# A planned instruction order for a spectral, soft-mixture and gated network: the planner gets other costs and a lock, weight conversions become twice as wide, and expert weights are loaded by POOL's queue

## The chip, the cores and the metric

The kernel runs on one core of one Trainium2 chip. A core has five engines that the text names as the profile does: PE (matrix products; PEld is its weight load), DVE (vector), ACT (scalar, with activation functions), POOL (GpSimd, elementwise work and DMA issue) and SP (used here only to issue DMAs). Each engine runs its own instructions in the order in which they were written and waits at an instruction until what it needs is ready. The metric is the time of one execution of the whole program in microseconds (us), the median of several runs. Before the change it is 1789.39 us, the median of 3 runs from 1787.84 to 1794.08 us.

## The reference

The reference has three parts, and all of it runs in one launch. `x` is 8 batches of 3072 tokens with 256 channels.

```
X  = rfft(x, axis=1);  Xr, Xi = X.real, X.imag
Yr = Xr @ w_r - Xi @ w_i + b_r;  Yi = Xr @ w_i + Xi @ w_r + b_i
Yr, Yi = soft threshold of both at lam = 0.01
x  = irfft(Yr + 1j*Yi, n=3072, axis=1).reshape(8*3072, 256)

logits = x @ phi                                  # 32 slots, 4 for each of 8 experts
d = softmax of logits over all 24576 tokens;  c = softmax over the 32 slots
slot_input = d.T @ x;  slot_out[e] = relu(slot_input[e] @ w1[e]) @ w2[e]
x = c @ slot_out

out = (silu(x @ w_gate) * (x @ w_val)) @ w_out    # 256 -> 1536 -> 256
```

The three weights `w_gate`, `w_val` and `w_out` come as 64-bit floats. The kernel reads them as pairs of 32-bit words, builds 32-bit floats from the bits on DVE and stores them to a scratch in DRAM.

## The kernel before

The program has two halves. The **first half** (the function `phase1`) goes through the 8 batches. For each batch it loads `x` (`load_x`, tiles `xq`), transforms it in two stages of matrix products (`stage_a` into `chan`, lines 623 and 628; `stage_c` from `chan` into `xg` and `sf`/`sg`, lines 645 to 686), multiplies by the complex weights in three products (`stage_b`, line 740, into the PSUM tiles `pb`), adds bias, thresholds (`after_b`, lines 793 to 812, tiles `r` and `yt`), and turns and spreads the result (`stage_q`, lines 838 to 864, tiles `yt` and `yi`). `stage_c` to `stage_q` go in three groups for each batch, so there are 24 groups. Then come the logits, the running column maximum, the exponentials and the sums over tokens that become the slots' inputs (`logits`, `slots`, lines 898 to 1171), and the softmax over slots (`combine`, lines 1187 to 1221), whose result goes to the DRAM scratch `c_scr`. A float32 value that goes into a fast matrix product is split in a rounded part and the rest; the rest is what the functions `lo`, `sum_lo`, `join` and `rest_w` compute or what POOL does for them.

Between these steps the first half converts the 64-bit weights (`narrow`, lines 1242 to 1284): load a piece of 256 columns into `cvi` (SP), build bits in three DVE instructions (`bits`, lines 1250 to 1252), square the high word on ACT (`size`, 1256), select on DVE (`value`, 1269), for `w_out` split the value (ACT 1272, POOL or DVE 1279), and store it (SP, 1284). There are 36 pieces, and `cvi` and `cv` have one buffer each, so a piece can only begin when the store of the one before has been read out of `cv`.

The order of all this isn't written by hand. `Plan.add` takes a task with its engine (or a choice of POOL and DVE), an assumed duration, a rank, the tiles that it reads and writes, and buffers that it takes. `Plan.run` then picks, again and again, the ready task that can start first on its engine; among equals the one with the lower rank. It adds `LAG` where a task follows one of another engine, and models SP's issue and the transfers for tasks with `bus`. The picked order is the order of the instructions in the program. Ranks get an offset from the table `SHIFT`. Nothing of the plan's times is in the program: only the order, and for the tasks with a choice the engine.

At the **end of the first half** the last batch has nothing beside it: after its last `stage_b` PE fills its waits with products of the identity (`hold`, line 1454, 80 of them), while the chain `stage_q`, `logits`, `slots` of the last batch goes from engine to engine. The expert weights `w1` (8 transfers of 1 MB, line 467) and `w2` (8 of 1 MB, line 472) are issued by SP as soon as the regions of the tiles `x`, `chan` and of the weights' splits are free, and so are two of the three loads of the converted gate weights (`wg`, line 480). In the **passage** (`after_slots`, lines 1476 to 1573) the sums are folded (1487 to 1494), the experts computed (1502 to 1525), and gate and value weights multiplied with their output (1587). The **second half** is one steady loop from line 1600 on: 576 steps of a gate product, a value product, silu, multiply, split and six products into the output.

## Time and profile before

| | |
|---|---|
| time of the program, median of 3 runs | 1789.39 us (1787.84 to 1794.08) |
| time of the profiled execution | 1793.57 us |
| its span, first to last instruction | 1791.4 us |
| PE busy over the span | 1710.6 us (95%) |
| DVE busy | 1329.6 us (74%) |
| ACT busy | 981.4 us (55%) |
| POOL busy | 275.0 us (15%), nearly all in the first half |
| mean granted TensorE clock | 0.983 |

A row of the view by stretches gives the stretch, then the busy time of each engine with its number of instructions, the granted clock, the mean share of the DMA engines and the GB/s. A row of the timeline gives start, duration, engine, line, operation, the tile written and the tiles read, how many were merged, and in brackets how long the engine had been idle before and what ended it. Idle time counts only on the engine whose work ends last in that stretch.

### The profile page before, as it was taken

What the parts mean: (1) busy time and instruction counts of PE and PEld (TensorE: products, weight loads), DVE (VectorE), ACT (ScalarE), POOL (GpSimd) and SP (SyncE); (2) the same over time, 40 slices, a digit from 0 to 9 for tenths busy, and PEclk for the clock granted to TensorE, in tenths of its full rate; (3) what the DMA queues carried; (4) which work ended last, traced back from release to release, by engine and by line L of the source; (5) the groups of instructions that cost most, each with busy time, mean ns of one, the idle gap of its engine ahead of it and who ended that gap; (6) DMA issues with size and microseconds to landing.
All of it is one profiled execution on the core that took longest, in us unless ns stands there. A gap on an engine that the chain in (4) does not pass through costs nothing.

```text
span 1791.4 us, 23405 instructions
## 1 busy us (share of the span) xinstructions
PE 1710.6 (95%) x8266; PEld 1300.9 (73%) x8266; DVE 1329.6 (74%) x2222; ACT 981.4 (55%) x1833; POOL 275.0 (15%) x254
## 2 busy tenths in 40 slices
PE   6999999899989777999999999999999999999998
PEld 3665676566757563788888888888888888888886
DVE  4688979888887652677777777777777777777776
ACT  1654556445556412566666555566666655566664
POOL 1334344334443432000000000000000000000000
PEclk9999999999999888999999999999999999999999
DMA  9357464573736479012112112113112113111111
GB/s 178 72 110 143 89 142 104 110 150 84 152 88 171 148 237 286 13 24 51 24 24 50 25 24 51 24 24 51 25 25 51 25 25 51 24 25 25 25 25 27
DMA packets 258915, 134.43 MB, mean 75 GB/s; under 512 B 197392, under 2 KB 246256, under 8 KB 258800
## 3 DMA queue, kind: packets, MB, share of 16 engines
q1 hardware_dynamic: 252944, 120.37, 31.6%
q0 software_dynamic: 5856, 12.58, 4.0%
q8 instruction: 65, 1.06, 0.3%
q14 instruction: 50, 0.41, 0.1%
HBM read 69.99 MB, written 37.75 MB: 60 GB/s over the span
## 4 chain that ended last, share of the span: by engine, by line
PE 81%; DVE 12%; DMA 1%; issue 1%; SPq 1%; ACT 1%; POOL 0%; DVEq 0%; ACTq 0%
PE o L1628 45%; PE pg L1603 7%; PE pv L1604 7%; PE pb L740 7%; PE ac L623 4%; PE ac L645 3%; PE ch L1100 1%; DVE yt L854 1%; PE ch L1152 1%; PE ch L838 1%; DVE xg L667 1%; DVE cv L1251 1%; DVE chan L628 1%; DVE vpad L884 1%; PE pb L1454 1%
## 5 line engine op out<-in xcount | busy, mean ns | idle before, releaser
L1628 PE MATMUL o<-hh,wo 128*128 128x512 f32 x2304 | 723.4, 395 | 0.0
L1608 DVE TENSOR_TENSOR h<-sg,pv 128x512 f32<-128x512 f32 x576 | 394.0, 684 | 273.5 <-ACT sg L1606 271.7
L1606 ACT ACTIVATE sg<-pg 128x512 f32<-128x512 f32 x576 | 344.8, 599 | 423.4 <-PE pg L1603 423.4
L1628 PEld LDWEIGHTS o<-hh,wo 128*128 128x128 f32 x2304 | 434.9, 189 | 100.9
L1628 PE MATMUL o<-hl,wo 128*128 128x512 f32 x1152 | 454.2, 394 | 0.0
L1616 DVE TENSOR_TENSOR hl<-h,hh 128x512 fp32r<-128x512 f32 x576 | 393.6, 683 | 0.1
L1615 ACT ACTIVATE hh<-h 128x512 fp32r<-128x512 f32 x576 | 359.3, 624 | 0.8 <-DVE h L1608 0.7
L1628 PEld LDWEIGHTS o<-hl,wo 128*128 128x128 f32 x1152 | 216.4, 188 | 51.9
L1603 PE MATMUL pg<-cst,gstk 96*128 96x512 f32 x576 | 228.6, 397 | 0.0
L1604 PE MATMUL pv<-cst,gstk 96*128 96x512 f32 x576 | 226.6, 393 | 0.9 <-DVE gstk L1590 0.7
L812 POOL TENSOR_TENSOR yt<-r,yt 128x512 f32<-128x512 f32 x92 | 119.3, 1297 | 249.0 <-ACT yt L803 194.3
L740 PE MATMUL pb<-xg,wh 128*128 128x512 f32 x384 | 148.2, 465 | 9.4 <-DVE xg L667 4.1
L1555 POOL DMA_DIRECT2D cst<-c_scr x24 | 13.6, 570 | 810.8 <-PE pv L1604 799.6
L1604 PEld LDWEIGHTS pv<-cst,gstk 96*128 96x128 f32 x576 | 109.9, 191 | 27.7 <-DVE gstk L1590 1.6
L1603 PEld LDWEIGHTS pg<-cst,gstk 96*128 96x128 f32 x576 | 108.2, 188 | 24.5 <-issue 0.5
L623 PE MATMUL ac<-xq,fwd 96*128 96x512 f32 x224 | 111.4, 606 | 4.6 <-DVE chan L628 2.4
L628 DVE STREAM_TRANSPOSE chan<-ac 128x512 f32<-128x512 f32 x128 | 88.7, 703 | 35.7 <-PE ac L623 32.7
L645 PEld LDWEIGHTS ac<-cm,chan 128*128 128x128 f32 x768 | 100.6, 200 | 17.7 <-issue 6.4
L645 PE MATMUL ac<-cm,chan 128*128 128x128 f32 x768 | 105.6, 288 | 3.2 <-DVE xg L667 1.7
L740 PEld LDWEIGHTS pb<-xg,wh 128*128 128x128 f32 x384 | 68.0, 193 | 48.6 <-issue 19.6
L667 DVE TENSOR_TENSOR xg<-ac,xg 128x512 fp32r<-128x512 f32 x96 | 64.9, 680 | 23.7 <-ACT sf L670 14.8
L740 PE MATMUL pb<-xg,wl 128*128 128x512 f32 x192 | 77.1, 401 | 0.0
(146 smaller groups left out, 1633.1 us busy)
## 6 DMA issues: line engine op xcount, KB each, us to landing
yi<-yt SPq DMA_DIRECT2D x384, 64.0 KB, 2.1
out_dram<-ob SPq DMA_DIRECT2D x192, 128.0 KB, 2.8
xq<-in_x_dram SPq DMA_DIRECT2D x28, 768.0 KB, 7.2
cst<-c_scr POOLq DMA_DIRECT2D x24, 384.0 KB, 5.8
w1s<-in_moe_w_dram SPq DMA_DIRECT2D x8, 1024.0 KB, 7.5
w2s<-in_moe_w_dram SPq DMA_DIRECT2D x8, 1024.0 KB, 8.7
w_scr<-cv SPq DMA_DIRECT2D x48, 128.0 KB, 3.2
x<-in_x_dram SPq DMA_DIRECT2D x2, 1536.0 KB, 15.5
```

The lines of the kernel that those rows point to most:

```text
L623: nc.tensor.matmul(out=pt, lhsT=fwd[:, 8 - 8 * dh:136 - 8 * dh], rhs=T[kq][:, :, d1:d1 + 16], start=True, stop=True)
L628: nc.vector.transpose(out=chan[:, 12 * dh:12 * dh + 16, d0:d0 + 16, :].rearrange("p j d i -> p d j i"), in_=T[ka].rearrange("p n d -> p d n"),
L645: nc.tensor.matmul(out=pt[:, :, q:q + 2, i // 2, :], lhsT=chan[:, 16 * dh + j // 2, :, j % 2], rhs=cm[:, j, :].rearrange("p (c h k) -> p c ...
L740: nc.tensor.matmul(out=pt, lhsT=w[:, dh, m, es], rhs=xx, start=m != 1 and dh == 0 and n == 0, stop=dh == 1 and n == 2, skip_group_check=True,)
L812: e.tensor_sub(out=part(), in0=quarters(T[kr]), in1=part())
L1603: nc.tensor.matmul(out=pg, lhsT=gstk[:, 0, f * 128:(f + 1) * 128], rhs=rhs, start=True, stop=True)
L1604: nc.tensor.matmul(out=pv, lhsT=gstk[:, 1, f * 128:(f + 1) * 128], rhs=rhs, start=True, stop=True)
L1606: nc.scalar.activation(out=sg, in_=pg, func=AF.Silu)
L1608: nc.vector.tensor_mul(out=h, in0=sg, in1=pv)
L1615: nc.scalar.activation(out=hh, in_=h, func=AF.Copy)
L1616: nc.vector.tensor_sub(out=hl, in0=h, in1=hh.bitcast(F32))
L1628: nc.tensor.matmul(out=po_t[0][k], lhsT=w[:, f % 4, k * 128:(k + 1) * 128], rhs=a, start=(f == 0 and m == 0), stop=(f == NF - 1 and m == 2 ...
```

## The change

- **Costs.** A table `COST` replaces the durations that `add` is called with, by the name of the function, for nearly every task of the first half. Most DVE and ACT durations rise (0.6 to 0.68 for `stage_c.lo`, 0.6 to 0.71 for `stage_a.turn`). `LAG` falls from 0.25 to 0.07. `SHIFT` stays as it was.
- **Lock.** The names in `PAIR` are DVE tasks that the planner lets run only when no POOL task runs, and the reverse. This is a rule for the planned order; no wait is added to the program.
- **Wider conversions.** A piece has 512 columns: 18 pieces instead of 36. A piece of `w_out` takes 256 rows of 256 columns, two rows to a partition, and is stored with four DMAs.
- **Weights by POOL.** `w1` and `w2` are issued from POOL, and their tasks no longer wait for one another. The last `w2` is placed behind the last batch's first group; the loads `wg` wait for it in the plan.

```
+COST = {
+    "stage_c.lo": {"DVE": 0.681},
...
+    "narrow.rest": {"POOL": 1.28, "DVE": 0.68},
+}
+PAIR = {
+    "mix_w", "rest_w", "stage_c.sum_lo", "after_b.join", "logits.join", "logits.spread", "logits.newmax",
+    "slots.cross", "slots.rot", "slots.join", "narrow.bits", "narrow.value", "narrow.rest",
+}
...
-    LAG = 0.25
+    LAG = 0.07
...
-            "eng": eng if isinstance(eng, dict) else {eng: dur}, "rank": rank, "fn": fn, "bus": bus,
+            "eng": COST.get(name, eng if isinstance(eng, dict) else {eng: dur}),
+            "rank": rank, "fn": fn, "bus": bus, "pair": name in PAIR,
...
+        def pair(t, eng):
+            return not t["bus"] and (eng == "POOL" or eng == "DVE" and t["pair"])
...
-                    start = max(free.get(eng, 0.0), can)
+                    start = max(free.get(eng, 0.0), can, lock if pair(t, eng) else 0.0)
...
+            if pair(t, eng):
+                lock = stop
...
-        nc.sync.dma_start(out=w1_t[e], in_=w1[e].rearrange("(k p) f -> p k f", p=128))
+        nc.gpsimd.dma_start(out=w1_t[e], in_=w1[e].rearrange("(k p) f -> p k f", p=128))
...
-        nc.sync.dma_start(out=w2_t[e], in_=w2[e].rearrange("(k p) f -> p k f", p=128))
+        nc.gpsimd.dma_start(out=w2_t[e], in_=w2[e].rearrange("(k p) f -> p k f", p=128))
...
-                t = sb(chp, ki, [128, 256, 2], "cvi", dt=I32)
-                nc.sync.dma_start(out=t.rearrange("p c t -> p (c t)"), in_=src)
+                t = sb(chp, ki, [128, 512, 2], "cvi", dt=I32)
+                nc.sync.dma_start(out=t.rearrange("p (u c) t -> p u (c t)", u=src.shape[1]), in_=src)
...
-            add("SP", 0.06, rank, load, w=[ki], new=("cvi", ki), bus=0.73, after=[("ac", "a", b, 15)])
-            add("DVE", 1.1, rank + 0.3, bits, w=[ki, ka], new=("cv", ka))
+            add("SP", 0.06, rank, load, w=[ki], new=("cvi", ki), bus=1.46, after=[("ac", "a", b, 15)])
+            add("DVE", 2.0, rank + 0.3, bits, w=[ki, ka], new=("cv", ka))
...
-            for k in range(0, rows, 128):
-                for c in range(0, cols, 256):
+            for k in range(0, 256, 128):
+                for c in range(0, FD, 512):
...
+        for k in range(0, FD, 256):
+            two = [w[k:k + 256].rearrange("(u p) f -> p u f", u=2) for w in (w32, *w_scr[2:4])]
...
-                "SP", 0.06, TT - 2.5 + 0.1 * e, fetch_w1(e), r=["w1a" if e < 3 else "w1b"], w=[("w1", e)], bus=2.91,
-                after=[("w1", e - 2)] if e > 1 else [],
+            add("POOL", 0.6, TT - 2.5 + 0.1 * e, fetch_w1(e), r=["w1a" if e < 3 else "w1b"], w=[("w1", e)], bus=2.91)
+        add(
+            "POOL", 0.6, TT - 1.5, fetch_w2(E - 1), w=["w2x"], new=("yi", "w2x"), bus=2.91, after=[("yi", last, 0, 0)],
+        )
...
-                "SP", 0.06, TT + 0.1 * e, fetch_w2(e), r=["w2p"], w=[("w2", e)], bus=2.91,
-                after=[("w2", e - 2) if e > 1 else ("w1", e + 6)],
+            add("POOL", 0.6, TT + 0.1 * e, fetch_w2(e), r=["w2p"], w=[("w2", e)], bus=2.91)
```

Line numbers of the first half are higher by 89 to 91 after the change (DVE's line 1250 becomes 1340, PE's 1502 becomes 1593).

**DVE in the last batch's slots.** This is the stretch from the row maximum `rm` to the sums `rs`: `vt` is the turned product, `vpad` its rotation, `cv` a conversion. Before:

```order
L1187 TENSOR_REDUCE rm<-ls 96x32
L1250 TENSOR_SCALAR cv<-cvi 128x256
L1251 SCALAR_TENSOR_TENSOR cv<-cvi,cv 128x256
L1252 SCALAR_TENSOR_TENSOR cv<-cvi,cv 128x256
L1064 STREAM_TRANSPOSE vt<-ch 128x512
L884 TENSOR_TENSOR vpad<-vt,csm 128x16x24
L1269 SCALAR_TENSOR_TENSOR cv<-cvi,cv 128x128 x2
L1064 STREAM_TRANSPOSE vt<-ch 128x512
L884 TENSOR_TENSOR vpad<-vt,csm 128x16x24
L1199 TENSOR_REDUCE rs<-ls 96x32
```

After:

```order
L1277 TENSOR_REDUCE rm<-ls 96x32
L1154 STREAM_TRANSPOSE vt<-ch 128x512 x2
L974 TENSOR_TENSOR vpad<-vt,csm 128x16x24 x2
L1289 TENSOR_REDUCE rs<-ls 96x32
L1290 TENSOR_SCALAR rs<-rs 96x32
```

The conversion's four rows are gone from between `rm` and the second `vt`.

**DVE at the passage.** From the last batch's sum `acc` to the folded sums `tail`. Before:

```order
L1208 STREAM_TRANSPOSE vt<-ls 96x1024
L1171 SCALAR_TENSOR_TENSOR acc<-acc,fac,ch 128x258
L1250 TENSOR_SCALAR cv<-cvi 128x256
L1251 SCALAR_TENSOR_TENSOR cv<-cvi,cv 128x256
L1252 SCALAR_TENSOR_TENSOR cv<-cvi,cv 128x256
L1269 SCALAR_TENSOR_TENSOR cv<-cvi,cv 128x128 x2
L1250 TENSOR_SCALAR cv<-cvi 128x256
L1251 SCALAR_TENSOR_TENSOR cv<-cvi,cv 128x256
L1252 SCALAR_TENSOR_TENSOR cv<-cvi,cv 128x256
L1269 SCALAR_TENSOR_TENSOR cv<-cvi,cv 128x128 x2
L1490 COPY tail<-pst 128x64
L1493 TENSOR_SCALAR tail<-pr 128x1
```

After:

```order
L1179 TENSOR_TENSOR vpad<-vpad,p_5478 128x16x12 x4
L1298 STREAM_TRANSPOSE vt<-ls 96x1024
L1261 SCALAR_TENSOR_TENSOR acc<-acc,fac,ch 128x258
L1581 COPY tail<-pst 128x64
L1584 TENSOR_SCALAR tail<-pr 128x1
```

Two conversions stood between `acc` and `tail`; now none does, and in the whole program no conversion stands behind the last batch's `stage_c`.

**POOL at the end of the first half.** `p` is a product for the rotation, `ls` the logits' softmax, `yt<-r,yt` the threshold's join, `sg` the rest of a sum. Before (no loads of `w1` and `w2` are on POOL):

```order
L812 TENSOR_TENSOR yt<-r,yt 128x4x128 x4
L1279 TENSOR_TENSOR cv<-cv 128x256
L812 TENSOR_TENSOR yt<-r,yt 128x4x128
L1190 TENSOR_TENSOR ls<-ls,rm 96x1024
L884 TENSOR_TENSOR p_5620<-vt,csm 128x384 x2
L1279 TENSOR_TENSOR cv<-cv 128x256
L1204 TENSOR_TENSOR ls<-ls,rs 96x1024
```

After:

```order
L776 TENSOR_TENSOR sg<-sf,sg 128x4x64
L557 DMA w1s<-in_moe_w_dram 128x2x1024 x5
L902 TENSOR_TENSOR yt<-r,yt 128x4x128
L562 DMA w2s<-in_moe_w_dram 128x8x256
L902 TENSOR_TENSOR yt<-r,yt 128x4x128 x4
L562 DMA w2s<-in_moe_w_dram 128x8x256 x7
L1280 TENSOR_TENSOR ls<-ls,rm 96x1024
L974 TENSOR_TENSOR p_5478<-vt,csm 128x384 x2
L1294 TENSOR_TENSOR ls<-ls,rs 96x1024
```

Fourteen of the 16 loads now stand here, seven of them ahead of the last batch's `ls` and `p`. Over the whole program POOL has 95 rows of `sg` and 95 of `yt<-r,yt` (72 and 92 before) and DVE one of each (24 and 4 before).

## Rows read from the trace of the kernel before

**Rows 1.** Busy time by stretch: columns as told above, PE first.
```profile
38.00:624.00 586.00, 549.79 (x3070) 378.36 (x3070) 480.65 (x848) 312.80 (x637) 234.91 (x203) 0.97 0.55 119
624.00:666.00 42.00, 37.07 (x296) 31.16 (x294) 26.23 (x46) 10.13 (x18) 14.45 (x10) 0.92 0.71 215
666.00:681.00 15.00, 0.45 (x4) 0.20 (x8) 3.28 (x12) 1.71 (x4) 0.79 (x2) 0.54 1.05 349
...
711.00:1791.00 1080.00, 1073.80 (x4610) 869.44 (x4609) 796.08 (x1249) 643.33 (x1152) 10.01 (x18) 1.00 0.19 31
```

**Rows 2.** Timeline of PE, 645 to 689 us.
```profile
645.36 1.88 PE L1056 MATMUL ch<-td,csm 96*128 96x512 f32 x4
647.08 3.96 PE L1454 MATMUL pb<-ident 128*128 128x128 f32 x34
654.50 2.90 PE L1100 MATMUL ch<-vpad,csm 128*128 128x192 f32 x8 [3.46 <-DVE vpad L1089]
...
680.55 5.53 PE L1502 MATMUL ph<-w1s,tail 128*32 128x512 f32 x32 [14.86 <-DVE tail L1493]
...
686.59 1.92 PE L1502 MATMUL ph<-w1s,tail 128*32 128x512 f32 x16
```

**Rows 3.** Timeline of DVE, 664 to 681 us.
```profile
664.32 0.48 DVE L1171 SCALAR_TENSOR_TENSOR acc<-acc,fac,ch 128x258 f32<-128x258 f32 x1 [2.16 <-PE ch L1152]
...
678.56 0.29 DVE L1250 TENSOR_SCALAR cv<-cvi 128x256 int32<-128x256 int32 x1 [11.15 <-DMA w_scr<-cv]
...
680.27 0.22 DVE L1490 COPY tail<-pst 128x64 f32<-128x64 f32 x1
```

**Rows 4.** Timeline of SP's queue at 668 us (DMA issues).
```profile
668.40 4.20 SPq L1284 DMA_DIRECT2D w_scr<-cv  x2
```

**Rows 5.** Timeline of DVE in the last batch's slots.
```profile
648.47 0.71 DVE L1064 STREAM_TRANSPOSE vt<-ch 128x512 f32<-128x512 f32 x1
...
649.69 1.29 DVE L1269 SCALAR_TENSOR_TENSOR cv<-cvi,cv 128x128 f32<-128x128 f32 x2
```

**Rows 6.** Timeline of PE at 137 us: the product of 654.50 in an earlier batch.
```profile
137.86 1.57 PE L1100 MATMUL ch<-vpad,csm 128*128 128x192 f32 x8 [0.39 <-DVE vpad L1089]
```

**Rows 7.** Timeline of POOL, 628 to 646 us.
```profile
628.87 0.73 POOL L1279 TENSOR_TENSOR cv<-cv 128x256 f32<-128x256 f32 x1 [0.93 <-POOL yt L812]
...
645.90 1.91 POOL L1190 TENSOR_TENSOR ls<-ls,rm 96x1024 f32<-96x1024 f32 x1 [15.08 <-ACT td L1038]
```

**Rows 8.** One line at a time: count, duration ns min/median/max, first and last start.
```profile
L1251 DVE SCALAR_TENSOR_TENSOR cv<-cvi,cv x36: 424/426/2087, 39.4 to 678.9; 128x256 int32<-128x256 int32 x36
L1555 POOL DMA_DIRECT2D cst<-c_scr x24: 562/562/730, 693.0 to 1513.4; - x24
L1546 POOL DMA_DIRECT2D wo<-w_scr x6: 745/760/787, 694.9 to 700.4; - x6
```

**Rows 9.** Groups by line: busy us, mean ns of one, then idle before.
```profile
L1251 DVE SCALAR_TENSOR_TENSOR cv<-cvi,cv 128x256 int32<-128x256 int32 x36 | 24.5, 682 | 1.2
L1269 DVE SCALAR_TENSOR_TENSOR cv<-cvi,cv 128x256 f32<-128x256 f32 (+1 forms) x48 | 23.0, 499 | 0.3
L686 DVE TENSOR_TENSOR sg<-sf,sg 128x256 fp32r<-128x256 f32 x24 | 18.0, 758 | 7.6 <-ACT sg L682 7.5
L1252 DVE SCALAR_TENSOR_TENSOR cv<-cvi,cv 128x256 int32<-128x256 int32 x36 | 17.5, 486 | 1.2
L1250 DVE TENSOR_SCALAR cv<-cvi 128x256 int32<-128x256 int32 x36 | 15.8, 439 | 12.1 <-DMA w_scr<-cv 11.2 <-DMA cvi<-in_moe_w_gate_dram 0.9
L555 DVE SCALAR_TENSOR_TENSOR wmix<-wst 128x512 f32<-128x512 f32 x1 | 0.7, 685 | 0.0
```

**Rows 10.** What PE waited for, 38 to 624 us: total us, times, longest.
```profile
PE ch L1100 <- DVE vpad L1089: 8.5, 6, 5.0
PE pb L740 <- DVE xg L667: 4.1, 6, 1.0
```

**Rows 11.** Timeline of PE at the start.
```profile
26.51 1.98 PE L623 MATMUL ac<-x,fwd 96*128 96x512 f32 x4 [2.22 <-DVE chan L628]
```

More of the change, by code (lines that the diff above doesn't have):

```diff
@@ L286 @@
+PAIR = {
+    "mix_w",
+    "rest_w",
+    "stage_c.sum_lo",
+    "after_b.join",
+    "logits.join",
+    "logits.spread",
+    "logits.newmax",
+    "slots.cross",
+    "slots.rot",
+    "slots.join",
+    "narrow.bits",
+    "narrow.value",
+    "narrow.rest",
+}
 class Plan:
-    LAG = 0.25
+    LAG = 0.07
     HAND, SET, SEEN = 0.65, 0.9, 0.65
@@ L310, in add @@
     def add(self, eng, dur, rank, fn, r=(), w=(), new=None, bus=0.0, dmas=1, after=()):
-        name = [n for n in fn.__qualname__.replace("<locals>.", "").split(".")[-3:] if n not in ("go", "phase1")]
+        name = [n for n in fn.__qualname__.replace("<locals>.", "").split(".")[-3:] if n not in ("go", "phase1", "kernel")]
         name = ".".join(name[-2:])
@@ L1282, in store @@
                 af, pf = (T[(*ka, n)].bitcast(F32) for n in "ap")
-                for o, t in zip(dst, (pf,) if len(dst) == 1 else (af, pf)):
-                    nc.sync.dma_start(out=o, in_=t)
-            add("SP", 0.06, rank, load, w=[ki], new=("cvi", ki), bus=0.73, after=[("ac", "a", b, 15)])
-            add("DVE", 1.1, rank + 0.3, bits, w=[ki, ka], new=("cv", ka))
-            add("ACT", 0.3, rank + 0.3, size, w=[ki])
-            add("DVE", 0.36, rank + 0.3, value, w=[ki, ka])
+                if len(dst) == 1:
+                    nc.sync.dma_start(out=dst[0], in_=pf)
+                    return
@@ new lines, in store @@
+                for o, t in zip(dst, (af, pf)):
+                    t = t.rearrange("p (h u x) -> p u h x", h=2, u=2)
+                    for u in range(2):
+                        nc.sync.dma_start(out=o[:, u].rearrange("p (h x) -> p h x", h=2), in_=t[:, u])
+            add("SP", 0.06, rank, load, w=[ki], new=("cvi", ki), bus=1.46, after=[("ac", "a", b, 15)])
+            add("DVE", 2.0, rank + 0.3, bits, w=[ki, ka], new=("cv", ka))
+            add("ACT", 0.5, rank + 0.3, size, w=[ki])
+            add("DVE", 0.65, rank + 0.3, value, w=[ki, ka])
@@ L1290, in narrow @@
             if len(dst) == 2:
-                add("ACT", 0.3, rank + 0.3, part, w=[ka])
-                add({"POOL": 0.69, "DVE": 0.34}, 0, rank + 0.3, rest, w=[ka])
-            add("SP", 0.12, rank + 0.4, store, r=[ka], w=[("ws", i)], bus=0.37 * len(dst), dmas=len(dst))
+                add("ACT", 0.5, rank + 0.3, part, w=[ka])
+                add({"POOL": 1.23, "DVE": 0.6}, 0, rank + 0.3, rest, w=[ka])
+            add("SP", 0.12, rank + 0.4, store, r=[ka], w=[("ws", i)], bus=0.74 * len(dst), dmas=len(dst) ** 2)
@@ L1446, in phase1 @@
                 "SP", 0.12, TT + 0.9, fetch_wg(t), w=[("wg", t)], bus=2.91, dmas=2, new=("yt", ("wg", t)),
-                after=[("ws", i) for i, (_, d) in enumerate(jobs) if len(d) == 1] + [("yi", last, 2, 0), ("w2", E - 2)],
+                after=[("ws", i) for i, (_, d) in enumerate(jobs) if len(d) == 1] + [("yi", last, 2, 0), ("w2", E - 2), "w2x"],
             )
@@ L1460, in phase1 @@
             add(
-                "PE", 0.22, TT + 50, hold(i), w=[kh], new=("pb", kh) if i == 0 else None,
+                "PE", 0.224, TT + 50, hold(i), w=[kh], new=("pb", kh) if i == 0 else None,
                 after=[("pb", last, 2, eh, d, 0) for eh in range(2) for d in range(2)],
```

84 lines of the change are left out of this document (68 added, 16 removed).

## The prediction

> **What bounds the kernel now.** I read the busy time by stretches first. From 711 us on PE is busy 1073.8 of 1080 us at a granted clock of 1.00 [rows 1]; the change issues nothing there, so only the first 711 us can move. In 38 to 624 us, the body, PE is busy 549.8 of 586 us and DVE 480.7 (82%) [rows 1]: PE bounds, with 36.2 us in which it waits. From 624 to 666 us the last batch's chain runs alone, with identity products in PE's waits; from 666 to 681 us PE does 0.45 us of work [rows 1].
>
> The timeline of PE, read next, shows that hole as one wait of 14.86 us, put down to DVE's `tail` [rows 2]. The timeline of DVE says why: `acc` is done at 664.80, but `tail` begins at 680.27, because two pieces of the conversion stand between them in DVE's order, and the second waits 11.15 us for a store out of `cv` [rows 3]. SP issued those stores at 668.40 and took 4.20 us for two [rows 4], with the loads of `w2` ahead of them in its queue. Nothing in the passage needs that piece so early. So 14.86 us are a place in DVE's order, not a dependency.
>
> **The change part by part.** The profiled execution took 1793.57 us (span 1791.4 and 2.2 around it); the median shown is 1789.39, so 4.2 lower. The sum is made against the former and taken off the latter.
>
> *The hole.* No conversion stands between `acc` and `tail` any more. PE ended its own part 14.86 us before 680.55, at 665.69; after it come only `tail` and its two followers, 0.28 us by the same rows (680.27 to 680.55) [rows 2, 3]. So the experts' product starts at about 666.0: **-14.5 us**. What is late next is `wg`, needed only behind all of the experts' products. It is now issued right behind the softmax's stores, no longer behind `w2`; I cost it at nothing, and it would cost what it lands late.
>
> *The clock behind the hole.* The stretch 666 to 681 us shows a granted clock of 0.54, thus mostly the level of 1.2 GHz, and the first 32 of the experts' products take 5.53 us, while 16 later ones take 1.92 [rows 1, 2]. At the later pace 32 take 3.84, so up to 1.7 is won; without the wait I take **-1.5**.
>
> *The last batch's slots.* The first half of PE's product at 645.36 is done by about 646.3, but the first `vt` begins at 648.47, behind a conversion; a second conversion step holds DVE from 649.69 for 1.29 us [rows 2, 5]. Both are gone, up to 2.2 + 1.3 = 3.5 us. PE waits 3.46 us there [rows 2], but the order now puts 24 identity products after that product, where there were 17 (34 instructions, 3.96 us [rows 2]): 7 more are 1.6 us, and only **-1.8** is left. With that wait short, the 8 products that took 2.90 us at 654.50 can run as at 137.86, where they took 1.57 [rows 2, 6]; there are two such sets, so up to 2.6 is won, bounded below by nothing: **-2**.
>
> *The last join.* A conversion of 0.73 us on POOL stands ahead of the last join [rows 7]: **-0.7**.
>
> *The weights on POOL.* Sixteen issues come into POOL's order. The trace shows issues of 384 and 512 KB there, at 562 and 760 ns median [rows 8]; for 1 MB I estimate by that slope about 1 us, and at most twice 760 ns. Seven stand ahead of the last batch's `ls`: 7 to 10.6 us from about 631 (the last join, begun behind the conversion at 628.87, is over by then) to 642 at the latest. POOL sat idle for 15.08 us before 645.90 [rows 7], and that `ls` can come some 3 us earlier now: covered, **0**. If the cover went, `ls` and `p` would come late by up to 6. The five `w1` issues ahead of a join are some 3 to 5 us, with the same chance of being waited for; I leave them in the body's range. SP loses 16 issues and 18 of its piece loads, and keeps 36 piece stores of 48.
>
> The Trainium skill (SBUF — State Buffer, section "SBUF: two separate sides") warns that while DVE holds the port that it shares with GpSimd, POOL cannot write the descriptors of its DMAs. The rows speak against it here: the 24 issues of `cst`, nearly all in a stretch in which DVE is 74% busy, take 562 ns at the median and 730 at most [rows 1, 8]. By the rule each of the seven would wait for one DVE instruction; what that gives is a rival below.
>
> *The conversions.* Before, the four DVE lines cost 15.8 + 24.5 + 17.5 + 23.0 = 80.8 us [rows 9]. `L1251` shows what is in that: 424 ns at least, 2087 at most [rows 8]; the long ones overlap POOL's work. Undisturbed, a piece of 256 costs about 0.28 + 0.42 + 0.42 + 0.41 = 1.5 us, 55 for 36. A 512-wide step costs at most the 685 ns of `L555` [rows 9]; a piece then is about 0.5 + 3 x 0.685 = 2.5 us, 46 for 18. So DVE loses between 9 (only starts) and 35 us (waits too). POOL takes 23 more rests of sums; at 758 ns each [rows 9] DVE loses another 17. Together 26 to 52 of 481 us. None of it lies on PE's path by itself.
>
> *The order in the body.* This can't be summed from rows. What can be won is bounded by PE's 36.2 us of waits; 10 of the 15 listed pairs wait for DVE, together 26.5 us, the largest 8.5 and 4.1 [rows 10]. If DVE has up to a tenth less to do and the planned order keeps its pairs off POOL's work, I take some 30% of those 26.5: **-8**. The other end: ranks fitted to other costs now break other ties, and the new DVE costs are the profile's durations, in which neighbours overlap a little, so the planner thinks DVE slower than it is. I take +36 (PE's waits double) as that end, and -36 as the other; -8 is nearer to nothing than to either, since PE's own work there, 549.8 us, doesn't change.
>
> *The start.* DVE stops for the weights' sums after 8 transposes, not 7, and the rest of one split (`wl`) goes to POOL. PE waits 2.22 us there [rows 11]; one product is worth about 1 there (1.98 us for two, of two instructions each), the split's rest some more, and I take **-1.5** between 0 and -2.2.
>
> Sum: -14.5 - 1.5 - 1.8 - 2 - 0.7 - 8 - 1.5 = -30.0. On the profiled execution 1763.6, on the median 1759.4. The runs shown spread 6 us, and I set **1761 us**.
>
> **The rivals.**
>
> *Only the passage moves.* The body's waits stay at 36: the planner's better numbers are evened out by ranks that were not refitted, and the pairs still collide, since the lock is no wait in the program. Then DVE's short conversions lie beside a PE that was bound elsewhere. For it: DVE is not the bound; against: most of PE's waits name it. -30 + 8 = -22, about 1767; with a body worse by up to 14 it reaches 1781.
>
> *POOL becomes the gate (the slower side).* `r` has one buffer: ACT's next threshold waits until POOL's join has read it, and PE's next `stage_b` waits until ACT has emptied `pb`. POOL now has nearly every rest and join, each longer than DVE's, and loads in its queue that wait for a freed region with a join behind them. If in each of the 24 groups a POOL result comes later than PE needs it by x, the body grows by 24x. It outweighs -22 of the other terms and the 5.4 of the bound for "slower" from x = 1.14 us on; at x = 1.5 the time is 1789 - 22 + 36 = 1803. For it: POOL's join is in the chain of every group. Against: POOL is busy 234.9 of 586 us [rows 1], and a quarter more leaves it half idle.
>
> *The shared port holds the issues.* By the skill's rule above, each of the seven `w2` issues would wait for one DVE instruction, up to 1.2 us for the longest in that chain (two steps at 649.69 took 1.29 together [rows 5]): 8.4 us more on POOL, `ls` at about 650 and some 7 us later than needed; the hole's gain stays. -30 + 7 gives 1766. If instead POOL's queue cannot take 7 MB at once, POOL stands until part has been moved, at 349 GB/s [rows 1] 3 us per MB; three MB gives about the same.
>
> **How the numbers follow.** Forecast 0.60 (its own range 1747 to 1770), only the passage 0.22, the held issues 0.06, POOL as gate 0.10, a body better by over 20 us 0.02. The range 1743 to 1782 takes in the forecast, the held issues and nearly all of the passage alone; outside are the gate and the far ends, some 0.17. A run of this kernel can tell 0.3% (5.4 us) from no change: faster is below 1784. That holds for all but the gate and a small end of the passage case: faster 0.83; the gate splits into slower 0.10, and same has 0.07.
>
> **What would show it.** Right: in the new trace the experts' first product follows the folded sums within about 1 us, with no conversion behind the last `acc`; the 32 first products take under 4.5 us; PE's idle time in the body is below 36 us, and the body is some 8 us shorter; the `L1341` durations have a smaller spread over their least value. Wrong: a wait of PE above 2 us between 624 and 711 us that ends with a POOL instruction or with a landing of `w2` or `wg`; POOL's `ls` of the last batch late behind its DMA issues; or a body longer than 586 us, with ACT's waits for `r` or PE's for `pb` grown, in which case the gate's delay for each group decides how much of the passage's gain is left.

## The result and the profile after

The changed kernel takes 1768.97 us (median of 4 runs, 1767.65 to 1769.84), the kernel before 1788.62 us (4 runs beside it, 1787.76 to 1794.08): a ratio of 0.988, with a 95% interval from 0.9858 to 0.9902. That is 19.7 us faster, where 28 were forecast. One execution among all those below (of the kernel "last two pieces late, first try") took 2818.9 us at a granted clock of 0.557 and is left out of its median.

| | before | after |
|---|---|---|
| span of the profiled execution | 1791.4 us | 1768.0 us |
| PE busy over the span | 1710.6 us (95%) | 1704.9 us (96%) |
| DVE busy | 1329.6 us | 1276.0 us |
| POOL busy | 275.0 us | 307.8 us |
| first product of the first `stage_c` | 33.95 us | 34.81 us |
| end of the last `stage_b` product | 624.50 us | 615.27 us |
| first product of the experts | 680.55 us | 659.24 us |
| from there to the span's end | 1110.9 us | 1108.8 us |

The lines of the table split the difference of the spans, -23.4 us: the start +0.9, the body (590.5 to 580.5) -10.1, the passage from the last `stage_b` to the experts (56.1 to 44.0) -12.1, and everything behind that -2.1. Lines of the changed kernel are 89 to 91 higher than those of before.

The view by stretches of the changed kernel, to be read beside [rows 1]:

```profile
36.00:615.00 579.00, 546.80 (x3089) 373.46 (x3089) 438.80 (x765) 318.38 (x626) 264.61 (x238) 0.99 0.56 124
615.00:647.00 32.00, 31.41 (x261) 26.88 (x263) 19.20 (x34) 8.03 (x14) 16.70 (x14) 1.00 1.04 323
647.00:659.00 12.00, 3.99 (x42) 2.13 (x30) 0.53 (x2) 0.81 (x1) 4.08 (x2) 0.73 1.04 356
690.00:1768.00 1078.00, 1071.71 (x4609) 868.74 (x4607) 795.44 (x1248) 642.78 (x1150) 10.02 (x18) 1.00 0.19 31
```

In the body DVE is busy 42 us less and PE waits 32.2 us instead of 36.2. Over the exact bodies, first the kernel before and then the changed one, the same view gives:

```profile
33.95:624.50 590.55, 553.46 (x3098) 381.79 (x3098) 483.29 (x853) 314.98 (x642) 236.13 (x204) 0.97 0.55 119
34.81:615.27 580.46, 548.26 (x3100) 374.81 (x3099) 439.51 (x766) 318.44 (x626) 264.88 (x238) 0.99 0.56 124
```

So the 10.1 us are two halves: PE waits 32.2 us instead of 37.1, and its products take 548.3 us instead of 553.5, at a mean granted clock of 0.99 instead of 0.97. The steady half is as it was. But there is a hole again, from 647 to 659 us, and from 615 on the DMA engines are full (1.04). The timeline of PE shows which product waits (compare [rows 2]):

```profile
641.88 1.47 PE L1190 MATMUL ch<-vpad,csm 128*128 128x192 f32 x8
643.51 1.57 PE L1190 MATMUL ch<-vpad,csm 128*128 128x192 f32 x8
...
646.42 1.49 PE L1242 MATMUL ch<-yi,p 128*32 128x256 f32 x23
655.33 1.93 PE L1242 MATMUL ch<-yi,p 128*32 128x256 f32 x16 [7.42 <-DMA c_scr<-td]
...
659.24 5.32 PE L1593 MATMUL ph<-w1s,tail 128*32 128x512 f32 x32
...
665.08 1.92 PE L1593 MATMUL ph<-w1s,tail 128*32 128x512 f32 x16
```

The timeline of DVE shows what has become of the old hole [rows 3]:

```profile
657.32 0.48 DVE L1261 SCALAR_TENSOR_TENSOR acc<-acc,fac,ch 128x258 f32<-128x258 f32 x1 [10.66 <-PE ch L1242]
658.96 0.22 DVE L1581 COPY tail<-pst 128x64 f32<-128x64 f32 x1 [1.16 <-PE pst L1578]
```

Between `acc` and `tail` there are 1.16 us where there were 15; the old hole is gone. In its place the last 16 slot products wait 7.42 us. The releaser that stands there, `c_scr`, is a store that these products don't read. They read `yi`, and the line that issues `yi` (SP, 21 issues from 620 us on) has this:

```profile
L954 SPq DMA_DIRECT2D yi<-yt x21: 585/585/1077, 620.0 to 645.7; - x21
...
who waited for it (us, times):
  PEld ch L1242: 7.9, 1
...
DMA to landing us min/median/max: 9.2/9.8/10.6
```

Over the whole program before, `yi` landed in 2.1 us at the median; in the same stretch of that kernel (629 to 656 us, 18 issues, with `w2` in the same queue) it was 6.5, and nobody waited. Here seven `w2` of 1 MB run beside it, which POOL has handed over all at once, as its timeline shows:

```profile
620.85 6.14 POOL L562 DMA_DIRECT2D w2s<-in_moe_w_dram  x7
635.80 1.90 POOL L1280 TENSOR_TENSOR ls<-ls,rm 96x1024 f32<-96x1024 f32 x1 [8.80 <-ACT td L1128]
```

And the line of these issues, with its durations in ns:

```profile
L562 POOL DMA_DIRECT2D w2s<-in_moe_w_dram x8: 882/883/927, 607.5 to 626.1; - x8
```

POOL itself is not late: an issue costs 0.88 us, and `ls` still waited for ACT. What is left is the data; a run below tests that. The seven `w2` are not alone: the ten `yi` issued from 611.4 to 620.0 us, ahead of them, already took 9.0 us at the median, beside the five `w1` and one `w2` that POOL had issued from 602.65 us on.

### The profile page after: what moved, and what is told of

Its sections match the earlier page's. It is cut to its first block, busy times and chain, and to the rows that moved or that the text cites. A ratio compares the mean times of both kernels' runs of the same rounds, so it can differ in the third digit from the quotient of the medians.

```text
span 1768.0 us, 23212 instructions
## 1 busy us (share of the span) xinstructions
PE 1704.9 (96%) x8266; PEld 1292.7 (73%) x8266; DVE 1276.0 (72%) x2116; ACT 981.8 (56%) x1809; POOL 307.8 (17%) x292
## 4 chain that ended last, share of the span: by engine, by line
PE 89%; DVE 5%; ACT 2%; DMA 1%; issue 1%; SPq 1%; POOL 0%; DVEq 0%; ACTq 0%; POOLq 0%
PE o L1719 45%; PE pb L830 9%; PE pg L1694 8%; PE pv L1695 8%; PE ac L713 6%; PE ac L735 4%; PE ch L928 1%; PE pb L1545 1%; PE ch L1242 1%; PE ch L1054 1%; PE ch L1190 1%; PE ch L988 1%; PE ch L1146 1%; PE pg L1678 1%; SPq L673 0%
## 5 line engine op out<-in xcount | busy, mean ns | idle before, releaser
L902 POOL TENSOR_TENSOR yt<-r,yt 128x512 f32<-128x512 f32 x95 | 124.9, 1315 | 223.8 <-ACT yt L893 124.5
L1646 POOL DMA_DIRECT2D cst<-c_scr x24 | 13.5, 566 | 818.9 <-PE pv L1695 797.9
L718 DVE STREAM_TRANSPOSE chan<-ac 128x512 f32<-128x512 f32 x128 | 88.1, 702 | 38.1 <-PE ac L713 35.3
L757 DVE TENSOR_TENSOR xg<-ac,xg 128x512 fp32r<-128x512 f32 x96 | 65.4, 683 | 27.4 <-ACT sf L760 15.2
L776 POOL TENSOR_TENSOR sg<-sf,sg 128x256 fp32r<-128x256 f32 x95 | 71.0, 757 | 64.3 <-ACT sg L772 54.4
```

Source lines behind the costliest of these rows:

```text
L718: nc.vector.transpose(out=chan[:, 12 * dh:12 * dh + 16, d0:d0 + 16, :].rearrange("p j d i -> p d j i"), in_=T[ka].rearrange("p n d -> p d n"),
L902: e.tensor_sub(out=part(), in0=quarters(T[kr]), in1=part())
```

## The experiments

Three theories were open. *The lock*: the body gains because the planner keeps DVE's paired operations off POOL's. *The durations*: it gains because the planner knows better how long things take. *The widening*: it gains because DVE has less to do. And for the passage: the new wait is w2's data on POOL's queue, or it is something else.

All runs in one table, in the order of the text. "Body" is the time from the first `stage_c` product to the end of the last `stage_b` product, "passage" from there to the experts' first product, both from the profiled execution. Each ratio is to runs of the kernel before that were made beside that kernel; the medians of these lie between 1788.62 and 1790.75 us.

| kernel | median us | ratio to before (95%) | body | passage |
|---|---|---|---|---|
| before | 1788.62 | | 590.5 | 56.1 |
| changed | 1768.97 | 0.988 (0.9858 to 0.9902) | 580.5 | 44.0 |
| changed, no lock, old durations | 1794.98 | 1.0025 (1.0013 to 1.0038) | 604.5 | 44.1 |
| changed, no lock | 1807.60 | 1.0093 (1.0076 to 1.011) | 618.0 | 43.2 |
| changed, old durations | 1763.14 | 0.9849 (0.9829 to 0.9869) | 575.6 | 42.6 |
| before, wide conversions only | 1797.59 | 1.0038 (1.0023 to 1.0052) | 604.8 | 35.3 |
| before, lock only | 1778.09 | 0.9927 (0.9911 to 0.9942) | 587.1 | 39.2 |
| before, lock and wide | 1760.41 | 0.9841 (0.9816 to 0.9867) | 580.9 | 34.5 |
| changed, narrow conversions | 1775.20 | 0.9914 (0.9893 to 0.9935) | 588.3 | 43.6 |
| before, last two pieces late, first try | 1794.84 | 1.0029 (1.0015 to 1.0043) | 586.6 | 38.5 |
| before, last two pieces late, second try | 1793.85 | 1.0024 (1.001 to 1.0039) | 589.2 | 40.1 |
| changed, w2 late | 1775.28 | 0.9909 (0.9893 to 0.9926) | 581.0 | 35.8 |
| changed, three w2 late | 1766.76 | 0.987 (0.9846 to 0.9894) | 581.1 | 42.9 |
| changed, old durations, three w2 late | **1757.86** | 0.9809 (0.9788 to 0.983) | 576.2 | 38.0 |

The body's time has a spread of its own: the two kernels with the last pieces late have the same order of instructions as the kernel before up to 620 us, and the three bodies lie between 586.6 and 590.5 us.

### The lock and the durations

Three kernels fill the square of "lock or not" and "old or measured durations", all with wide conversions and POOL's queue. Without both (cuts are marked with `...`; durations that the change had altered in three other lines go back too):

```diff
-PAIR = {
-    "mix_w",
-    "rest_w",
...
-}
+PAIR = set()
...
-    LAG = 0.07
+    LAG = 0.25
...
-            "eng": COST.get(name, eng if isinstance(eng, dict) else {eng: dur}),
+            "eng": eng if isinstance(eng, dict) else {eng: dur},
```

> The changed kernel with the old durations of the planner, the old lag and no lock: wide conversions and weights by POOL's queue alone. Theory (of the body's 10.1 us most comes from DVE's conversions, 80.8 to 54.4 us of busy time, and little from the planner's better numbers; the hole goes by the widening too, since no piece is left over at the end): 1768 to 1774 us, body of 580 to 585 us. Rival (the body's gain is the measured durations'): body back at 588 to 592 us, time 1777 to 1782 us.

Neither came: 1794.98 us, slower than before. With the measured durations, without the lock (only the first edit, `PAIR = set()`):

> The changed kernel with the measured durations but with no operation marked as one of the pair, so that the planner puts POOL's operations and VectorE's paired ones side by side. Theory (the two engines hold each other up for what the durations already contain, and the lock only reorders): within 0.3% of the changed kernel, 1764 to 1774 us. Rival (without the lock DVE's paired operations wait for POOL's port beyond their measured durations): body 5 to 10 us longer, time 1774 to 1780 us.

It took 1807.60 us, beyond the rival too. And with the lock, on the old durations (all but the first edit, so "durations" here always means `COST` and `LAG` together):

> The changed kernel with the lock but with the old durations and the old lag in the planner; with the three other cells (neither: 1794.98, measured durations alone: 1807.6, both: 1768.97 us) this tells the lock from the durations. Theory (the lock carries the gain, since the durations alone lost 12.6 us against neither): within 1764 to 1777 us. Rival (only both together are right, because the lock needs to know when POOL ends): 1782 to 1795 us.

1763.14 us: 0.9 us better than the theory's range, and far from the rival's. So the lock is worth 31.8 us on the old durations (1794.98 to 1763.14) and 38.6 on the measured ones. The measured durations cost 12.6 us without the lock, and 5.8 with it; in the latter case the two intervals overlap, but the runs don't (1762.89 to 1763.78 against 1767.65 to 1769.84). Most of it is body: 604.5, 618.0, 575.6 and 580.5 us.

What the lock takes away can be seen in one place of the kernel without it (no lock, old durations). DVE's timeline at 412 us:

```profile
412.42 2.32 DVE L1165 TENSOR_TENSOR vpad<-vpad,p 128x192 f32<-128x192 f32 x2
```

POOL's, at the same time:

```profile
412.58 1.95 POOL L1266 TENSOR_TENSOR ls<-ls,rm 96x1024 f32<-96x1024 f32 x1 [1.62 <-DVE rm L1263]
```

And PE's, which is waiting for DVE:

```profile
414.80 1.34 PE L1176 MATMUL ch<-vpad,csm 128*128 128x192 f32 x6 [1.33 <-DVE vpad L1165]
```

Two additions of the same shape take 0.62 us undisturbed, in the kernel with the lock and the old durations:

```profile
407.06 0.62 DVE L1009 TENSOR_TENSOR vpad<-vpad,p 128x192 f32<-128x192 f32 x2
```

Here they take 2.32, from 412.42 to 414.74, and POOL's `ls` runs from 412.58 to 414.53: DVE stands until POOL is done, and PE waits for it 1.33 us. The Trainium skill (SBUF — State Buffer, section "SBUF: two separate sides") says that DVE and GpSimd share a port pair that is an exclusive lock and no shared bandwidth: an operation of DVE with two inputs in SBUF, or one of GpSimd, has it for the whole instruction, and the other is blocked. These rows agree: 2.32 us is about one addition of 0.3 and POOL's 1.95 on top. So the planner's lock puts into the order what the machine does anyway. Over the whole first half, the line of the same additions and of another set like it, in the kernel before (count, ns min/median/max, first and last start):

```profile
L1089 DVE TENSOR_TENSOR vpad<-vpad,p x32: 291/344/2066, 133.5 to 654.8; 128x192 f32<-128x192 f32 x32
L919 DVE TENSOR_TENSOR vpad<-vpad,p x32: 314/352/1442, 107.2 to 637.7; 128x192 f32<-128x192 f32 x32
```

The same two lines in the changed kernel:

```profile
L1179 DVE TENSOR_TENSOR vpad<-vpad,p x32: 291/348/1460, 147.5 to 641.8; 128x192 f32<-128x192 f32 x32
L1009 DVE TENSOR_TENSOR vpad<-vpad,p x32: 316/352/361, 111.2 to 627.6; 128x192 f32<-128x192 f32 x32
```

The medians are the same; the tails are shorter or gone. PE's largest wait in the list of its waits, for these `vpad` ([rows 10]; 12.4 us in 12 waits without lock and durations, 36 to 600 us), has left the list of the changed kernel.

```profile
PE ch L1176 <- DVE vpad L1165: 12.4, 12, 3.3
```

Over the whole body DVE is busy 484.1 us without the lock and 442.0 with it on the old durations, 484.4 and 439.5 on the measured ones. Not all of that is meetings avoided. With the lock the planner also gives POOL nearly all the rests of sums (`sg`): DVE has 26 and 27 of them in the two bodies without it, 18.1 and 22.0 us, and one in each with it. The 56 additions into `vpad` show the meetings apart from that, since DVE does the same ones in all four bodies: 36.8 us without the lock and 23.1 with it on the old durations, 30.4 and 20.7 on the measured ones. How much of the 32 to 39 us comes from the one and how much from the other wasn't tested.

Why the measured durations cost time stays open. What PE waits for in 36 to 600 us (total us, times, longest), in the changed kernel:

```profile
PE ch L1054 <- DVE vt L1017: 8.6, 7, 2.2
PE pb L830 <- DVE xg L757: 4.4, 4, 1.8
PE pb L830 <- ACT yt L883: 3.9, 6, 1.3
```

And with the lock and the old durations:

```profile
PE pb L830 <- ACT r L893: 5.0, 5, 2.3
PE pb L830 <- DVE xg L757: 4.0, 5, 2.1
PE pb L830 <- ACT yt L883: 4.0, 5, 1.5
PE ch L1054 <- DVE vt L1017: 3.1, 2, 1.9
```

DVE's turned `vt` is late seven times instead of two; other waits are shorter. Over the whole bodies PE waits 32.2 and 30.4 us, and its products take 548.3 and 545.2 us, so most of the 4.9 us of body is not in the waits. The ranks stayed as they had been set for the old durations; whether ranks set anew would turn the loss into a gain wasn't tried.

### The widening

The widening alone, on the kernel before:

```diff
-                t = sb(chp, ki, [128, 256, 2], "cvi", dt=I32)
+                t = sb(chp, ki, [128, 512, 2], "cvi", dt=I32)
...
-            add("DVE", 1.1, rank + 0.3, bits, w=[ki, ka], new=("cv", ka))
+            add("DVE", 2.0, rank + 0.3, bits, w=[ki, ka], new=("cv", ka))
...
```

> The kernel before with the wide conversions alone: 18 pieces of 512 columns, old durations, no lock, w1 and w2 still by SP's queue. Its order on DVE in the last passage has no conversion behind the accumulators. Theory (it is the lock that gains; a wide piece beside POOL loses what it saves): the body as in the run with the old costs and no lock (1794.98 us), less that run's 7.38 us wait for yi, which needs w2 on POOL's queue: 1785 to 1790 us. Rival (the widening is worth what the prediction gave it, 8 us of body and the hole of 14.5 us): 1766 to 1772 us.

1797.59 us: slower than before, and beyond the theory. Its passage is the short one (no conversion behind `acc`, 35.3 us), but its body is 604.8 us. The lock alone, on the kernel before, with `PAIR` as in the change:

```diff
...
-                    start = max(free.get(eng, 0.0), can)
+                    start = max(free.get(eng, 0.0), can, lock if pair(t, eng) else 0.0)
...
+            if pair(t, eng):
+                lock = stop
```

> The kernel before with the lock alone: 36 pieces of 256 columns, old durations, w1 and w2 by SP's queue; one conversion piece is left between the accumulators and the tail on DVE, where there were two. Theory (the lock carries the body's gain, 10 us and more, and the hole falls to the 1.8 us of one piece since no second one waits for the first one's store): 1764 to 1774 us. Rival (with narrow pieces the lock delays POOL's operations, and so yt, by as much as DVE gains): 1782 to 1790 us.

1778.09 us, 4 above the theory's range and 4 below the rival's. The body is 3.4 us shorter, no more than the spread of the bodies told above; most of the gain is the hole, of which one piece of the conversion is left:

```profile
662.13 6.31 PE L1526 MATMUL ph<-w1s,tail 128*32 128x512 f32 x32 [2.42 <-DVE tail L1514]
```

Both together on the kernel before (weights still by SP):

> The lock and the wide conversions, with the old durations and with w1 and w2 on SP's queue as before, where yi's issues stand in one line with them. Theory (the run with lock, old durations and POOL's queue took 1763.14 us, 6.51 us of it at the slots for yi and 2.8 us in 32 cold products right behind; on SP's queue yi lands in 2 us): 1752 to 1757 us. Rival (w2, the last of it issued only behind c_scr, comes late for the second products): a wait of 4 to 9 us there, 1758 to 1764 us.

1760.41 us, the rival's time, but by other reasons: the first experts' product is warm and early (3.64 us at 647.96), `w2` comes only 0.97 us late and `wg` 1.4, and the body is 580.9 us and not the 575.6 that the theory took from the run before. So the widening costs 6.8 us without the lock (1790.75 to 1797.59, the kernel before as run beside it) and gains 17.7 with it (1778.09 to 1760.41). A reason can be seen in the additions into `vpad` that PE's products read (28 in each body). In the kernel before they take 610 ns on the mean, with the wide conversions alone 856, and PE's waits for them grow from 8.5 us in 6 waits to 13.2 in 13; with the lock alone they take 604, with both 483, and PE's waits for them are 6.6 and 1.9 us. So without the lock the wide pieces save DVE nothing: over the whole bodies it is busy 483.3 us before and 484.8 with the wide conversions, against 456.5 with the lock and 443.9 with both. PE's idle time in the same bodies is 37.1, 49.4, 41.9 and 33.7 us, and the granted clock 0.97, 0.97, 0.98 and 0.99. Why wide pieces bring more meetings about in the planned order wasn't tested.

This run answers one more question. It has the weights on SP's queue and is otherwise as the run with lock, old durations and POOL's queue: 0.9841 (0.9816 to 0.9867) against 0.9849 (0.9829 to 0.9869). The wide conversions without the lock, on SP's and on POOL's queue, are as close: 1.0038 (1.0023 to 1.0052) and 1.0025 (1.0013 to 1.0038). So moving `w1` and `w2` to POOL by itself gains nothing that these runs can tell.

From the other side, the changed kernel with narrow pieces:

> The changed kernel with the conversions back at 256 columns (36 pieces instead of 18, planned at half the durations: 1.15 us for the three bit operations, 0.4 for the value, 0.77 on POOL) and everything else of the change kept: the price of the widening where the lock is in force. Theory (half the columns take more than half the time: 282 to 426 ns against 381 to 694, so 36 pieces cost DVE some 10 us more in the body, a third of which TensorE feels): body 3 to 6 us longer, 1772 to 1776 us. Rival (DVE has room, TensorE is the bound of the body): within 3 us of the changed kernel.

1775.20 us with a body of 588.3: the time as in the theory, the body longer than it (7.8 us). So here the widening is worth 6.2 us.

### The hole

The kernel before, with the last two pieces taken out of the plan and put by hand behind the folded sums and behind the last turned tile:

```diff
...
+            if i >= len(jobs) - 2:
+                held.append([load, bits, size, value, part, lambda: rest("POOL"), store])
+                return
...
```

> The kernel before, with one edit: the last two conversion pieces are taken out of the planner's hands and put by hand behind the reciprocal of the last passage and behind its last turned tile, so that nothing of a conversion stands between the accumulators and the tail on DVE. All else is as before. Theory (the 14.86 us hole is a price of its own): 1788.6 - 14.5 = 1774 us, with the 16 tail products starting 14 us sooner; 1772.5 if the experts' 32 products are warm for it. Rival (something else comes nearly as late as the tail, w1, w2 or the tail's own operands): the hole shrinks by less than 8 us, time 1781 to 1785 us.

1794.84 us. Then with the loads on POOL's queue and all the arithmetic behind the last turned tile:

> The kernel before, with the last two conversion pieces out of the planner's hands: their loads go to POOL's queue at the experts' first products, and all their arithmetic stands on DVE and ACT behind the experts' four first products and turned tiles, so that no h1 waits for it (in the run before this one ACT's conversion, whose load landed at 685 us, stood ahead of h1 and cost 21.94 us). Theory (the 14.86 us hole is a price of its own): the first experts' product at 663 us instead of 680.55 and warm (3.64 instead of 5.53 us), psot at 699.94 - 17 = 683 us, time 1770 to 1774 us. Rival (w2, whose last issue stands at 670 us on SP, or wg behind it, comes late as soon as the products come early): 5 to 12 us of wait at the experts' second products or at wg, time 1778 to 1785 us.

Both were slower than before, and in both the edit itself is the reason. In the first ACT's square stood ahead of `h1` and waited for the piece's load (PE: 21.94 us). In the second it stood ahead of the experts' result on ACT. The timeline of PE in the second:

```profile
663.86 3.64 PE L1514 MATMUL ph<-w1s,tail 128*32 128x512 f32 x32
...
680.48 3.61 PE L1537 MATMUL po<-w2s,h1t 128*32 128x256 f32 x58 [2.43 <-DMA w2s<-in_moe_w_dram]
699.29 1.22 PE L1586 MATMUL psot<-fold,tail 128*128 128x128 f32 x4 [15.19 <-ACT tail L1582]
```

And of DVE:

```profile
696.57 0.29 DVE L1256 TENSOR_SCALAR cv<-cvi 128x256 int32<-128x256 int32 x1 [17.00 <-DMA w_scr<-cv]
```

Up to the last expert product the theory holds: it ends at 684.09 us, 15.2 before that of the kernel before (695.66 + 3.66), with 32 warm products at the start. Then the hole comes back, moved: the second piece waits 17.00 us for the store out of the one buffer `cv`, and all behind it waits too. The hole's price is shown, and so is its cause; that leaving those pieces out of the way gains it in the total isn't shown by these two runs, but by the lock alone, where the wait fell from 14.86 to 2.42 and the passage from 56.1 to 39.2 us.

### The weights on POOL's queue

The changed kernel with the first seven `w2` behind the last `yi`:

```diff
-            add("POOL", 0.6, TT + 0.1 * e, fetch_w2(e), r=["w2p"], w=[("w2", e)], bus=2.91)
+            add(
+                "POOL", 0.6, TT + 0.1 * e, fetch_w2(e), r=["w2p"], w=[("w2", e)], bus=2.91,
+                after=[("yi", last, 2, p) for p in range(4)],
+            )
```

> The changed kernel, with one edit: the first seven w2 transfers are handed to POOL's queue only after the four y tiles of the last group have been handed over, so that the tiles' landing has the DMA engines with less company; all eight w2 are still loaded. Theory (w2's 7 MB hold up the yi tiles, whose last landing holds TensorE for 7.42 us at the second batch of slot products): that wait falls below 1.5 us, the time to 1761 to 1763 us. Rival A (the bytes have to come in anyway; the wait only moves behind, to the experts' second products that read w2): no wait at the slots, but one of 5 to 8 us at w2, time 1767 to 1770 us. Rival B (the wait is for DVE's last gather and not for a landing): the wait stays at 7 us, time 1768 us.

The theory's half about the cause is right: `yi` lands in 2.1 us at the median, no product waits for it, and the experts start at 648.56 us, warm. The rival's half is right too, and larger than it said:

```profile
648.56 3.64 PE L1596 MATMUL ph<-w1s,tail 128*32 128x512 f32 x32
...
658.66 0.59 PE L1619 MATMUL po<-w2s,h1t 128*32 128x256 f32 x2 [2.88 <-DMA w2s<-in_moe_w_dram]
...
662.99 3.16 PE L1619 MATMUL po<-w2s,h1t 128*32 128x256 f32 x25 [3.74 <-DMA w2s<-in_moe_w_dram]
...
677.65 2.91 PE L1619 MATMUL po<-w2s,h1t 128*32 128x256 f32 x24 [5.33 <-DMA w2s<-in_moe_w_dram]
```

12 us of waits for `w2`, and 1775.28 us. Then only the last three of them, in the changed kernel:

```diff
...
+                after=[("yi", last, 2, p) for p in range(4)] if e > 3 else [],
...
```

> The changed kernel, with one edit: w2 of the first four experts goes to POOL's queue where the change puts it, w2 of the fifth to seventh only after the four y tiles of the last group have been handed over. Theory (a landing of yi takes 2 us when w2 is not under way and 9 us when it is, and the experts' second products need the first four w2 about 7 us before the other three): no wait at the slots, the first experts' product at about 649 us instead of 659.24, at most 2 us of wait at w2, time 1756 to 1760 us. Rival A (the wait moves to the last three w2, as all seven did in the run before this one): first product at 649 us, but 4 to 8 us of wait at w2, time 1763 to 1769 us. Rival B (4 MB early are enough to hold yi up): the wait at the slots stays above 4 us, time 1765 to 1769 us.

Rival B: the wait stays at 6.31 us. The time, 1766.76 us, can't be told from the changed kernel's. And the same edit with the old durations:

> The lock with the old durations, wide conversions and POOL's queue (1763.14 us), and w2 of the fifth to seventh expert handed over only after the last group's four y tiles. Theory (as between the changed kernel and its own run with this edit, 1768.97 to 1766.76 us, the wait for yi stays and only a little is won): 1760 to 1763 us. Rival (the body ends at another point here, so that yi is free of w2): the wait of 6.51 us goes, 1754 to 1757 us.

1757.86 us, with a wait of 1.99 us: between the theory and the rival, 0.9 us above the rival's range.

```profile
643.65 1.81 PE L1242 MATMUL ch<-yi,p 128*32 128x256 f32 x16 [1.99 <-DMA yi<-yt]
...
647.42 5.22 PE L1596 MATMUL ph<-w1s,tail 128*32 128x512 f32 x32
```

It has the lowest median, 11 us below the changed kernel with intervals that don't touch; the interval of lock and wide (0.9816 to 0.9867) overlaps its own. What differs between the two kernels with three late `w2`, besides the durations, is when the DMA engines are through with what was handed over first. In the one the five `w1` are issued at 600.05 us and the DMA share is 1.05 from 630 to 640 us; in the other at 593.67, and it is 0.67 there, when the last `yi` are handed over. No run moved the `w1` alone, so this is not shown to be the cause.

The Trainium skill (DMA: Bandwidth & Descriptors, section "Queues, rings and completion order") says that each DMA engine takes turns, packet by packet, between the queues that have work for it. The rows fit: a 64 KB `yi` on SP's queue gets through neither at once nor last when POOL's queue holds megabytes, but in 9.8 us instead of 2.1.

## Why the prediction was right or wrong

The direction and the range were right, the time 8 us too low. By its own steps:

| term | forecast | measured | |
|---|---|---|---|
| the hole | -14.5 | -14.5 | `tail` is 1.16 us behind `acc`; no conversion in between |
| clock behind it | -1.5 | -0.2 | 5.32 us for the 32 products, not 3.84 |
| last slots and last join | -2.5 | -3.4 | from the last `stage_b` to the first `L1190`: 30.0 to 26.6 |
| `L1190` warm | -2 | -2.9 | 1.47 and 1.57 us instead of 2.90 and 2.93 |
| weights on POOL | 0 | +8.7 | the wait for `yi`, 7.4, and 1.3 in the cold products behind it |
| order of the body | -8 | -10.1 | 590.5 to 580.5 |
| start | -1.5 | +0.9 | clock |
| behind the experts' first products | 0 | -1.9 | not looked for |
| sum | -30.0 | -23.4 | |

**The step that failed** is "covered, 0" for the weights on POOL. It priced POOL's time for the issues, and not too low: 7 issues took 6.14 us against an estimate of 7 to 10.6, and `ls` had to wait 8.80 us more for ACT's `td`. What it left out is what the issues start. Before, `w2` stood in one queue with `yi` on SP, in the order of the plan. On POOL's queue they are under way when the last `yi` are handed over, and those land in 9.8 us (6.5 in the same stretch before). The DMA share was already 1.05 in the old hole [rows 1], so the question "what will run beside these 7 MB" could have been asked from a row that was shown. The prediction said to look for a wait above 2 us that ends with a landing, but of `w2` or `wg`; it was `yi`, the small transfer. The run with `w2` later shows the cause by itself (2.1 us, no wait). It also shows that delaying all seven only moves the wait: 12 us for `w2` in place of 7.4 for `yi`, since the bytes have to come in.

**The clock's term** fell with it: the wait was only moved ahead of the experts. The granted clock is 0.73 from 647 to 659 us, and the products behind it take 5.32 us; where PE had no such wait ahead of them (w2 late, lock and wide, wide only, both tries at the hole), they took 3.64.

**The body** was right in size and not in its reason, so that the -8 came near the -10.1 is in part luck. The prediction gave it 30% of the waits that name DVE, since DVE would have less to do *and* the pairs would be kept off POOL, and it took the planner's better durations for a help with a risk. The runs separate these: the wide conversions without the lock make the body 14.3 us longer, the measured durations make it 13.5 longer without the lock and 4.9 with it. The lock turns the first round (587.1 to 580.9) and shrinks the second. The bound of +36 for other tie-breaks was no idle one: +27.5 is what the changed kernel's body has without the lock. And the bound by PE's waits left a term out: "PE's own work there, 549.8 us, doesn't change" does not hold. The waits fell by 4.9 us only; the other 5.2 are products that took less time at the higher granted clock, and in the kernel without lock on the measured durations, at 0.97, they took 562.2 us.

**The start**: PE's wait fell from 2.22 to 1.45 us [rows 11], as said, but the 12 products behind it took 8.91 us at a granted clock of 0.80 (19 to 36 us). In the two kernels that differ from the changed one only in when `w2` is issued, near 620 us, they took 5.86 in both, and the first `stage_c` came at 31.77 and 31.64 us, 2.2 and 2.3 earlier than before. The term was right for the order and missed what the clock does in one execution; how often it does so isn't known.

**The rivals.** POOL did not become the gate: PE's waits for `yt` of POOL are 1.6 us in the body. The held issues did not come either: 882 to 884 ns for the six `w2` issues with DVE at work beside them, 899 and 927 for the two others. The rule that the prediction took from the Trainium skill (SBUF — State Buffer, section "SBUF: two separate sides") names an operation of DVE in a two-port mode, which is narrower than the prediction's "holds the port". Whether any of the operations beside these issues ran in one, no run shows. "The pairs still collide, since the lock is no wait in the program" was wrong: the lock is in the order alone, and it gained 12.7 us by itself and 32 to 39 with wide conversions. The rival's other half has something in it: the new durations, on ranks not refitted, did cost time.

## What to carry to other kernels

Where DVE and POOL work side by side, plan their paired operations so that they don't meet before making them wider, fewer or better timed: here wider conversions lost 7 us and measured durations 13 without that, and the kernel with wide conversions gained 32 to 39 with it. When a transfer is moved to another engine's queue, price its data and not only its issue: ask which small transfer on another queue will be under way beside it, and who waits for that. When an engine bounds a stretch, look at its granted clock besides its waits: here half of what the body gained was there. And a part of a change that looks harmless by reason (measured durations in place of guesses) deserves a run of its own when ranks have been set to the old ones.

## What the runs showed of the hardware that was not expected

- A 64 KB transfer on SP's queue landed in 2.1 us at the median over the program, and in 9.8 us beside transfers of 1 MB on POOL's queue, with the DMA engines at a share of 1.04.
- An issue of 1 MB took POOL 883 ns at the median and 927 at most (`w2`), and 713 ns at the median and 889 at most (`w1`). The six `w2` issues with DVE at work beside them took 882 to 884 ns, the two without 899 and 927.
- The same instructions at the program's start took 8.91 us in one execution and 5.86 in another; the granted clock was 0.80 and 1.00 there.
- A wait of 1.99 us at the last slots was followed by 5.22 us instead of 3.64 in the 32 products of the experts; another of 2.43 us, for `w2` (second try at the hole), was followed by 58 products in 3.61 us, the same as behind a wait of 0.97 us (lock and wide). So the length of one wait did not decide it.
